# Layer A spectrum: the self-paired rows last, sums and differences on GpSimd, last evictions on two engines

## Chip, cores, metric

The kernel runs on one core of one Trainium2 chip. The metric is device time of one execution in microseconds (us). I call the TensorE matmul engine PE, VectorE DVE, ScalarE ACT, and GpSimd also POOL, as the profile does.

## The reference, cut to what matters

```python
def _A_ref(x, w_r, w_i):                       # x: 1 x 2048 x 640
    X = jnp.fft.rfft2(x.astype(jnp.float32), axes=(-2, -1))
    X = X * (w_r + 1j * w_i)                   # 2048 x 321 weights
    return jnp.fft.irfft2(X, s=(S, D), axes=(-2, -1)).astype(jnp.bfloat16)
...
x = x + _A_ref(_layernorm(x), ...)             # layer A1
x = x + _B_ref(_layernorm(x), ...)             # layer B1 (attention with memory; not changed)
x = x + _A_ref(_layernorm(x), ...)             # layer A2
x = x + _B_ref(_layernorm(x), ...)             # layer B2 (not changed)
```

Layer A is computed with matmuls against Fourier tables. Its middle, `spectrum()`, works through eight groups of rows. Group 0 holds the rows whose mirror is in the same group ("self-paired"); it needs fewer sums than the other seven. After it, `tokens()` needs the result of all eight groups, so the whole of `spectrum()` is on the critical path, in both layers A.

## The kernel before: the parts that matter

An eviction is the copy of a result of PE from PSUM to SBUF. All of this is in `spectrum()`; PE, ACT and DVE run in the order written, GpSimd in an order that a scheduler chooses (here also the order written).

```python
def along_d(j, o):          # 10 matmuls on PE into PSUM tile ab0 or ab1; for o == 1 ACT copies the result out
def combine(j):             # DVE: a+b and a-b, one operand in PSUM, one in SBUF (for j == 0 two copies, one on DVE, one on ACT)
def across(j, sg):          # PE: 4 matmuls into PSUM tile X, of which there is only one
def filt(j, sg):            # DVE: two multiplies of X (PSUM) by the weights (SBUF), into t1, t2
    ...
def products(j, sum_engine):
    sd[j] = quads[2 + j % 3]
    t1, t2 = ts[j % 2]
    a = sd[j].rearrange("p (c s) f -> p c s f", c=2) if j == 0 else acs[j % 2]
    nc.vector.tensor_tensor(out=a[:, 0, :, :], in0=t1[:, :, 0, :], in1=t2[:, :, 0, :], op=ALU.subtract)   # L326
    nc.gpsimd.tensor_tensor(out=a[:, 1, :, :], in0=t1[:, :, 1, :], in1=t2[:, :, 1, :], op=ALU.add)        # L327
    if j:
        sum_engine.tensor_tensor(out=sd[j][:, 0:2, :], in0=a[:, :, 0, :], in1=a[:, :, 1, :], op=ALU.add)  # L329
        nc.gpsimd.tensor_tensor(out=sd[j][:, 2:4, :], in0=a[:, :, 0, :], in1=a[:, :, 1, :], op=ALU.subtract)  # L330

def back(j):                # the inverse transform of group j
    for ch, (f0, f1) in enumerate(CH):                         # three chunks of the 321 frequencies
        psu = pp.tile([128, 2, 2, 128], FP32, tag="pu", bufs=2)  # one PSUM tile for both halves
        ...                                                    # 4 matmuls
        for e in range(2):                                     # two evictions of one half each
            nc.scalar.copy(out=UT[0:m, ch, e, :, j * 16:j * 16 + 16]..., in_=psu[0:m, e, :, :]...)

for j in range(8 + 3):
    if j < 8:       along_d(j, 1)
    if 1 <= j <= 8: across(j - 1, 0); filt(j - 1, 0)
    if j < 8:       along_d(j, 0); combine(j)
    if 1 <= j <= 8: across(j - 1, 1)
    if j >= 3:      back(j - 3)
    if 1 <= j <= 8: filt(j - 1, 1); products(j - 1, nc.vector if j >= 7 else nc.gpsimd)
```
(laid out more tightly than in the file; loads of weights and tables are cut)

Of the kernel before, what the change touches and what calls it, by code (L numbers as in the profile page):

```python
# [13 lines left out]
ALU = mybir.AluOpType  # L14
# [6 lines left out]
NF = 321  # L21
# [76 lines left out]
def _gate(nc, dst1, src1):  # L98
    nc.scalar.copy(out=dst1, in_=src1)
# [36 lines left out]
class _Cut:  # L136

    def __init__(self, t):
        self.t, self.o = t, 0
# [38 lines left out]

class LayerA:

    def __init__(self, tc, g, ar, w_r, w_i, lname):
        self.tc, self.g, self.ar, self.lname = tc, g, ar, lname
        self.w = (w_r, w_i)
        self.wv = [w.rearrange("(p g) f -> p g f", g=16) for w in self.w]
# [17 lines left out]
            nc.gpsimd.indirect_dma_start(out=self.Wm[:, i, :], out_offset=None, in_=w.rearrange("(p g) f -> p (g f)", g=16),  # L202
                                         in_offset=bass.IndirectOffsetOnAxis(ap=self.g["mirror"][:, 0:1], axis=0), element_offset=9 * NF)

    def load_w(self, j):
        nc, W = self.tc.nc, self.W
        W[j, 0] = self.wts[j % 3]
        if j:
            W[j, 1] = self.Wm[:, :, (7 - j) * NF:(8 - j) * NF]
        for i in range(2):  # L210
            nc.sync.dma_start(out=W[j, 0][:, i, :], in_=self.wv[i][:, j, :])
# [49 lines left out]
    def spectrum(self, late_loads=()):  # L261
        tc, g, YT, Fd, K = self.tc, self.g, self.YT, self.Fd, self.K
        nc, W = tc.nc, self.W
        self.UT = UT = self.ar.get("S3", f"{self.lname}UT").bf(3, 2, 16, 128)
        s1 = self.ar.get("S1", f"{self.lname}tmp")
        quads = [s1.bf(4, NF) for _ in range(5)]
        ts = [[s1.f32(2, 2, NF) for _ in range(2)] for _ in range(2)]
        dbs = s1.f32(2, NF)
        W[0, 1] = s1.bf(2, NF)
        for i in range(2):  # L270
            nc.sync.dma_start(out=W[0, 1][:, i, :], in_=self.wv[i][:, 8, :])
        s6 = self.ar.get("S6", f"{self.lname}gt")
        self.Gd = Gd = s6.bf(3, 2, NF)
        self.Ti = Ti = s6.bf(16, 2, 128)
        acs = [s6.f32(2, 2, NF) for _ in range(2)]
        late = [lambda gt: (_gate(nc, Gd[0:1, 0, 0, 0:1], gt), nc.sync.dma_start(out=Gd, in_=g["cd"]["cGd"]))]
        for hf in range(2):
            late.append(lambda gt, hf=hf: (_gate(nc, Ti[0:1, 8 * hf, 0, 0:1], gt),
                                           nc.sync.dma_start(out=Ti[:, 8 * hf:8 * hf + 8], in_=g["cd"]["cTi"][:, 8 * hf:8 * hf + 8])))
        late += list(late_loads)  # L280
        pp = tc.alloc_tile_pool(name=f"{self.lname}_ps2", bufs=1, space=PSUM)
        Kf = K.rearrange("p a b -> p (a b)")
        ab, P, X, sd = {}, {}, {}, {}
        CH = [(0, 128), (128, 256), (256, NF)]

        def along_d(j, o):
            ab[j, o] = ps = pp.tile([128, 2, 512], FP32, name=f"ab{o}", tag=f"ab{o}")
            for ch in range(5):
                for c in range(2):
                    nc.tensor.matmul(ps[:, 1 - c if o else c, 0:NF], lhsT=YT[:, ch, 2 * j + c, :, :].rearrange("p s k -> p (s k)"), rhs=Fd[:, ch, o, :],  # L290
                                     start=(ch == 0), stop=(ch == 4))
            if o == 1 and j:
                ab[j, o] = dbs
                nc.scalar.copy(out=dbs, in_=ps[:, :, 0:NF])

        def combine(j):
            P[j] = quads[j % 2]
            ac, db = ab[j, 0], ab[j, 1]
            if j == 0:
                nc.scalar.copy(out=P[j][:, 2:4, :], in_=db[:, :, 0:NF])  # L300
                nc.vector.tensor_copy(out=P[j][:, 0:2, :], in_=ac[:, :, 0:NF])
                return
            nc.vector.tensor_tensor(out=P[j][:, 0:2, :], in0=ac[:, :, 0:NF], in1=db, op=ALU.add)
            nc.vector.tensor_tensor(out=P[j][:, 2:4, :], in0=ac[:, :, 0:NF], in1=db, op=ALU.subtract)

        def across(j, sg):
            X[j, sg] = x = pp.tile([128, 2, 512], FP32, name="X", tag="X")
            if j == 0:
                a, b = (0, 3) if sg == 0 else (1, 2)
                k = 4 + 3 * sg  # L310
                ops = [(0, k, a), (0, k + 1, b), (1, k + 1, a), (1, k + 2, b)]
            else:
                ops = [(0, 2, 0), (0, 3, 3), (1, 2, 3), (1, 1, 0)] if sg == 0 else [(0, 2, 2), (0, 3, 1), (1, 0, 1), (1, 3, 2)]
            for i, (o, k, p) in enumerate(ops):
                nc.tensor.matmul(x[:, o, 0:NF], lhsT=K[:, k, :], rhs=P[j][:, p, :], start=(i % 2 == 0), stop=(i % 2 == 1))

        def filt(j, sg):
            x = X[j, sg]
            for t, xv, i in ((ts[j % 2][0], x[:, :, 0:NF], 0), (ts[j % 2][1], x[:, ::-1, 0:NF], 1)):
                nc.vector.tensor_tensor(out=t[:, sg, :, :], in0=xv, in1=W[j, sg][:, i, :].unsqueeze(1).to_broadcast([128, 2, NF]), op=ALU.mult)  # L320

        def products(j, sum_engine):
            sd[j] = quads[2 + j % 3]
            t1, t2 = ts[j % 2]
            a = sd[j].rearrange("p (c s) f -> p c s f", c=2) if j == 0 else acs[j % 2]
            nc.vector.tensor_tensor(out=a[:, 0, :, :], in0=t1[:, :, 0, :], in1=t2[:, :, 0, :], op=ALU.subtract)  # L326
            nc.gpsimd.tensor_tensor(out=a[:, 1, :, :], in0=t1[:, :, 1, :], in1=t2[:, :, 1, :], op=ALU.add)  # L327
            if j:
                sum_engine.tensor_tensor(out=sd[j][:, 0:2, :], in0=a[:, :, 0, :], in1=a[:, :, 1, :], op=ALU.add)  # L329
                nc.gpsimd.tensor_tensor(out=sd[j][:, 2:4, :], in0=a[:, :, 0, :], in1=a[:, :, 1, :], op=ALU.subtract)  # L330

        def back(j):
            for ch, (f0, f1) in enumerate(CH):
                m = f1 - f0
                psu = pp.tile([128, 2, 2, 128], FP32, name="psu2", tag="pu", bufs=2)
                if j == 0:
                    for c in range(2):
                        for part in range(2):
                            nc.tensor.matmul(psu[0:m, :, c, :], lhsT=sd[j][:, 2 * part + c, f0:f1], rhs=K[:, 10 + 4 * c + 2 * part:12 + 4 * c + 2 * part, :],
                                             start=(part == 0), stop=(part == 1))  # L340
                else:
                    for e, ops in enumerate((((0, 256), (3, 128)), ((1, 0), (2, 128)))):
                        for i, (o, k) in enumerate(ops):
                            nc.tensor.matmul(psu[0:m, e, :, :], lhsT=sd[j][:, o, f0:f1], rhs=Kf[:, k:k + 256], start=(i == 0), stop=(i == 1))
                for e in range(2):
                    nc.scalar.copy(out=UT[0:m, ch, e, :, j * 16:j * 16 + 16].rearrange("p s (c k) -> p s c k", c=2),
                                   in_=psu[0:m, e, :, :].rearrange("p c (s k) -> p s c k", k=8))

        with tc.manual_schedule(engines={nc.tensor.engine, nc.scalar.engine, nc.vector.engine}):
            for j in range(8 + 3):  # L350
                if j < 8:
                    along_d(j, 1)
                if 1 <= j <= 8:
                    across(j - 1, 0)
                    filt(j - 1, 0)
                if j < 8:
                    along_d(j, 0)
                    combine(j)
                if 1 <= j <= 8:
                    across(j - 1, 1)  # L360
                if j >= 3:
                    back(j - 3)
                    for _ in range(2):
                        if late:
                            late.pop(0)(UT[0:1, 0, 0, 0, (j - 3) * 16:(j - 3) * 16 + 1])
                if 1 <= j <= 8:
                    filt(j - 1, 1)
                    products(j - 1, nc.vector if j >= 7 else nc.gpsimd)
                    if j + 2 < 8:
                        self.load_w(j + 2)  # L370
            for f in late:
                f(UT[0:1, 0, 0, 0, 112:113])
        pp.release()
# [419 lines left out]
def _b_fast_pass(tc, g, bs, env, flag_col, nxt=None):  # L793
# [31 lines left out]
    if True:  # L825
# [196 lines left out]
        with tc.manual_schedule(engines={nc.tensor.engine, nc.scalar.engine, nc.vector.engine}):  # L1022
            for h in range(H + 2):
                if h < H and h % 2 == 0:
                    w = load_w(h // 2)
                    Vt[h // 2] = Vs[h // 2 % 2]
# [389 lines left out]
```

## Time and profile before

| | before |
|---|---|
| median of the first 3 runs | 1668.94 us |
| PE busy over the span | 94% |
| spectrum of A1 (PE starts it; tokens stage starts) | 36.15 to 99.40 us |
| spectrum of A2 | 852.29 to 914.88 us |
| one row group in mid stage | 6.72 us |

The page's first line and its first line on busy time (busy us, share, instructions of each engine):

```profile
span 1669.1 us, 36193 instructions
...
PE 1564.6 (94%) x14240; PEld 1081.5 (65%) x14241; DVE 810.9 (49%) x2308; ACT 837.0 (50%) x2534; POOL 268.5 (16%) x192
```

PE at 94% does not say that PE is the limit everywhere. The view of busy time by stretch, for the second spectrum (window, its length, then busy us and instructions of PE, weight loads, DVE, ACT, POOL, then granted clock, DMA share, GB/s):

```profile
852.00:915.00 63.00, 48.21 (x321) 32.18 (x322) 48.80 (x57) 20.75 (x60) 32.09 (x24) 0.94 0.13 39
```

PE and DVE are each busy for less than 49 of 63 us. What limits the stage must be read from who waits for whom. The DVE timeline of one row group (start, length, engine, line, operation, output from inputs, shape, count):

```profile
882.43 1.55 DVE L320 TENSOR_TENSOR A2tmp_S<-X,A2tab_S 128x642 f32<-128x642 f32 x2
883.90 0.81 DVE L303 TENSOR_TENSOR A2tmp_S<-ab,A2tmp_S 128x642 bf16<-128x642 f32 x1
884.64 0.81 DVE L304 TENSOR_TENSOR A2tmp_S<-ab,A2tmp_S 128x642 bf16<-128x642 f32 x1
885.37 1.54 DVE L320 TENSOR_TENSOR A2tmp_S<-X,A2tab_S 128x642 f32<-128x642 f32 x2
887.02 2.20 DVE L326 TENSOR_TENSOR A2gt_S<-A2tmp_S 128x642 f32<-128x642 f32 x1
889.14 1.55 DVE L320 TENSOR_TENSOR A2tmp_S<-X,A2tab_S 128x642 f32<-128x642 f32 x2
```

From first filter (L320) to first filter is 6.71 us. DVE has no gap over 0.1 us in it. L326, the difference of products, takes 2.20 us. GpSimd's timeline of the same time:

```profile
886.99 1.54 POOL L327 TENSOR_TENSOR A2gt_S<-A2tmp_S 128x642 f32<-128x642 f32 x1 [1.71 <-DVE A2tmp_S L320]
889.39 1.32 POOL L329 TENSOR_TENSOR A2tmp_S<-A2gt_S 128x642 bf16<-128x642 f32 x1 [0.85 <-DVE A2gt_S L326]
```

GpSimd's sum L327 started 0.03 us ahead of L326. Both operations read two tensors in SBUF. There are 16 such pairs in the two layers. In the eight in which DVE started ahead, for instance at 907.99 us below, L326 took 0.83 us and GpSimd's sum 2.05 to 2.21 us; in the eight in which GpSimd started ahead, by 0.02 to 0.03 us, the sum took 1.54 to 1.57 us and L326 2.20 to 2.22 us, ending 0.68 to 0.69 us after the sum. So the one that started second was the longer for it; below I say that it stalled.

The end of the stage, on DVE and on PE:

```profile
906.39 1.56 DVE L320 TENSOR_TENSOR A2tmp_S<-X,A2tab_S 128x642 f32<-128x642 f32 x2 [1.35 <-PE X L315]
907.99 0.83 DVE L326 TENSOR_TENSOR A2gt_S<-A2tmp_S 128x642 f32<-128x642 f32 x1
910.26 0.83 DVE L329 TENSOR_TENSOR A2tmp_S<-A2gt_S 128x642 bf16<-128x642 f32 x1 [1.44 <-POOL A2gt_S L327]
```

```profile
905.10 1.25 PE L315 MATMUL X<-A2tmp_S,A2tab_S 128*128 128x321 bf16 x4 [4.00 <-DVE A2tmp_S L320]
...
914.88 3.38 PE L393 MATMUL psg<-A2gt_S,A2UT_S 128*128 128x321 bf16 x12 [0.73 <-ACT A2UT_S L346]
```

The last filter starts at 906.39 us, the last products end at 912.26, and the tokens stage starts at 914.88 (L393). PE waited 4.00 us for the filter ahead of its last across-matmuls (L315), and these four took 1.25 us where they take 0.72 in mid stage.

### The profile page before, as it was taken

How to read it: one execution, taken by the hardware profiler on the slowest of the kernel's cores; microseconds unless marked ns; L12 is line 12 of the kernel's file. 1: busy time of each engine (PE TensorE's matmuls, PEld its weight loads, DVE VectorE, ACT ScalarE, POOL GpSimd, SP SyncE). 2: the span in 40 equal slices, each digit the busy share in tenths (PEclk: the TensorE clock that was granted, in tenths of full speed). 3: DMA queues.
4: the chain of work that ended last, by engine and by line, in shares of the span. 5: the costliest groups of instructions: out<-in, count | busy, mean ns of one | idle time of the engine just before them, and what ended most of it. 6: DMA issues, size and time to landing. Idle time of an engine off the chain costs nothing. (4 is left out here: it accounts for less than half of the span.)

```text
span 1669.1 us, 36193 instructions
## 1 busy us (share of the span) xinstructions
PE 1564.6 (94%) x14240; PEld 1081.5 (65%) x14241; DVE 810.9 (49%) x2308; ACT 837.0 (50%) x2534; POOL 268.5 (16%) x192
## 2 busy tenths in 40 slices
PE   4887999999999999999987889999999999999998
PEld 2555666666666666677754666676666666666775
DVE  5963354545555554543357724545555554544111
ACT  5364466666666666511123636666666666663000
POOL 0510111121212121100025001121212121111000
PEclk9997999999999999999999999999999999999999
DMA  4463134434343344633301803434343343437241
GB/s 154 158 237 104 51 137 135 151 114 162 112 161 127 137 147 139 227 129 100 91 17 58 283 2 106 148 116 162 112 160 129 135 149 136 136 123 233 66 127 55
DMA packets 167873, 218.05 MB, mean 131 GB/s; under 512 B 7374, under 2 KB 141836, under 8 KB 159756
## 3 DMA queue, kind: packets, MB, share of 16 engines
q1 hardware_dynamic: 167084, 213.34, 38.2%
q8 instruction: 113, 1.85, 0.4%
q0 software_dynamic: 608, 2.30, 0.4%
q14 instruction: 68, 0.56, 0.1%
HBM read 170.52 MB, written 45.09 MB: 129 GB/s over the span
## 5 line engine op out<-in xcount | busy, mean ns | idle before, releaser
L840 PEld LDWEIGHTS <-bB_S 128*128 128x128 bf16 x3180 | 260.3, 97 | 187.1 <-issue 7.8
L984 DVE TENSOR_TENSOR bB_S<-pso,bB_S 128x480 bf16<-128x480 f32 (+1 forms) x320 | 189.5, 593 | 264.7 <-PE pso L975 249.1
L919 ACT ACTIVATE bB_S<-pss 128x269 bf16<-128x269 f32 (+5 forms) x576 | 213.3, 385 | 192.6 <-PE pss L916 177.8
L1134 PE MATMUL psx<-Wo_sb,bB_S 128*128 128x320 bf16 x2048 | 288.2, 299 | 2.9 <-DMA bB_S<-oTx_d 2.9
L1134 PEld LDWEIGHTS <-bB_S 128*128 128x128 bf16 x2048 | 197.2, 98 | 79.5 <-DMA bB_S<-oTx_d 3.6
L899 DVE CAST bB_S<-psk 128x495 bf16<-128x495 f32 (+3 forms) x320 | 191.4, 599 | 115.9 <-PE psk L840 85.6
L920 DVE TENSOR_TENSOR bB_S<-bB_S,maskf 128x269 bf16<-128x269 bf16 (+5 forms) x576 | 163.1, 287 | 152.6 <-ACT bB_S L919 148.8
L944 POOL TENSOR_TENSOR bB_S<-bB_S,bB_S 128x634 f32<-128x634 f32 x64 | 98.2, 1535 | 821.1 <-ACT bB_S L940 821.1
L908 ACT CAST bB_S<-psv 128x512 bf16<-128x512 f32 (+1 forms) x288 | 160.5, 557 | 84.0 <-PE psv L906 83.7
L884 ACT ACTIVATE bB_S<-psq 128x480 bf16<-128x480 f32 x300 | 152.6, 509 | 98.2 <-PE psq L840 98.2
L840 PE MATMUL psk<-B2hT_S,bB_S 128*128 128x495 bf16 (+3 forms) x800 | 165.0, 342 | 3.7 <-DVE bB_S L899 2.5
L840 PE MATMUL psk<-B1hT_S,bB_S 128*128 128x495 bf16 (+3 forms) x800 | 165.0, 342 | 1.8 <-DVE B1hT_S L1219 1.2
L906 PE MATMUL psv<-bB_S,B2hT_S 128*128 128x256 bf16 x1360 | 163.4, 272 | 0.2 <-DVE bB_S L899 0.2
L906 PE MATMUL psv<-bB_S,B1hT_S 128*128 128x256 bf16 x1360 | 163.4, 272 | 0.2 <-DVE bB_S L899 0.2
L916 PEld LDWEIGHTS <-bB_S 128*128 128x128 bf16 x1216 | 103.0, 98 | 90.1 <-issue 6.4
L840 PE MATMUL psq<-B1hT_S,bB_S 128*128 128x495 bf16 (+5 forms) x780 | 157.6, 336 | 0.1
L840 PE MATMUL psq<-B2hT_S,bB_S 128*128 128x495 bf16 (+5 forms) x780 | 157.6, 336 | 0.1
L916 PE MATMUL pss<-bB_S 128*128 128x132 bf16 (+8 forms) x1216 | 148.3, 216 | 3.1
L906 PEld LDWEIGHTS <-B1hT_S 128*128 128x128 bf16 x1360 | 128.6, 98 | 13.7 <-issue 0.3
L906 PEld LDWEIGHTS <-B2hT_S 128*128 128x128 bf16 x1360 | 128.5, 98 | 13.8 <-issue 0.3
L975 PE MATMUL pso<-bB_S,bB_S 128*128 128x132 bf16 (+8 forms) x1216 | 119.6, 216 | 0.0
L975 PEld LDWEIGHTS <-bB_S 128*128 128x128 bf16 x1216 | 91.2, 98 | 15.7 <-DVE oTmf L985 0.5
(223 smaller groups left out, 1565.7 us busy)
## 6 DMA issues: line engine op xcount, KB each, us to landing
bB_S<-Rd SPq DMA_DIRECT2D x62, 1059.5 KB
oTx_d<-bB_S SPq DMA_DIRECT2D x60, 512.0 KB
bB_S<-oTx_d SPq DMA_DIRECT2D x56, 512.0 KB
bB_S<-in_B_Wq_dram SPq DMA_DIRECT2D x32, 320.0 KB
bB_S<-in_B_Wk_dram SPq DMA_DIRECT2D x32, 320.0 KB
bB_S<-in_B_Wv_dram SPq DMA_DIRECT2D x32, 320.0 KB
bB_S<-oTx_d SPq DMA_DIRECT2D x14, 384.0 KB
Wo_sb<-in_B_Wo_dram SPq DMA_DIRECT2D x4, 1280.0 KB
```

The source lines that it names most:

```text
L840: nc.tensor.matmul(ps, lhsT=w[:, ch, hh * 128:(hh + 1) * 128], rhs=src[:, ch, lo:hi], start=(ch == 0), stop=(ch == 4))
L884: nc.scalar.mul(out=qv[:, :, 0:SEG], in_=x_view(ps, o, n)[:, :, 1:SW], mul=scale)
L899: nc.vector.tensor_copy(out=KTs[h % 2][:, lo:hi], in_=ps[:, 0:hi - lo])
L906: nc.tensor.matmul(ps[:, i * 256:(i + 1) * 256], lhsT=hT[:, ch, (t + i) * 128:(t + i + 1) * 128], rhs=w["Wv"][:, ch, :], start=(ch == 0), ...
L908: nc.scalar.copy(out=V[:, t:t + n, :].rearrange("p a b -> p (a b)"), in_=ps[:, 0:n * 256])
L916: nc.tensor.matmul(ps[:, off - o0:off - o0 + hi - lo], lhsT=KT[:, t * 128:(t + 1) * 128], rhs=QT[:, lo:hi], start=True, stop=True)
L919: nc.scalar.activation(out=E[:, 0:n], in_=ps[:, 0:n], func=ACTF.Exp)
L920: nc.vector.tensor_tensor(out=P[:, o0:o0 + n], in0=E[:, 0:n], in1=bs.mask[:, o0:o0 + n], op=ALU.mult)
L944: nc.gpsimd.tensor_tensor(out=accS, in0=accS, in1=sums_sb, op=ALU.add)
L975: nc.tensor.matmul(pso[:, lo - q0:hi - q0], lhsT=V[:, t, (h % 2) * 128:(h % 2 + 1) * 128], rhs=P[:, off:off + hi - lo], start=(i == 0), st ...
L984: nc.vector.tensor_tensor(out=oT.rearrange("p (r s j) -> p r s j", r=16, j=2)[:, :, s0:s0 + ns, :], in0=byclass(po), in1=rx, op=ALU.mult)
L1134: self.tc.nc.tensor.matmul(ps[:, 0:320], lhsT=lhs(h, k // 2), rhs=self.g["Wo_sb"][:, h, c0:c0 + 320], start=(h == 0), stop=(h == H - 1))
```

## The change

The intent: take L326 from DVE in mid stage; let the last group be the self-paired one, which needs just two operations after its filters, on DVE; and divide the last evictions between ACT and DVE.

```diff
+    SEQ = (1, 2, 3, 4, 5, 6, 7, 0)
 ...
+        pos = {j: p for p, j in enumerate(self.SEQ)}
 ...
-        def products(j, sum_engine):
+        def products(j):
 ...
-            nc.vector.tensor_tensor(out=a[:, 0, :, :], ..., op=ALU.subtract)
-            nc.gpsimd.tensor_tensor(out=a[:, 1, :, :], ..., op=ALU.add)
+            (nc.gpsimd if pos[j] < 6 else nc.vector).tensor_tensor(out=a[:, 0, :, :], ..., op=ALU.subtract)
+            (nc.gpsimd if j else nc.vector).tensor_tensor(out=a[:, 1, :, :], ..., op=ALU.add)
             if j:
-                sum_engine.tensor_tensor(out=sd[j][:, 0:2, :], ..., op=ALU.add)
+                nc.gpsimd.tensor_tensor(out=sd[j][:, 0:2, :], ..., op=ALU.add)
                 nc.gpsimd.tensor_tensor(out=sd[j][:, 2:4, :], ..., op=ALU.subtract)
 ...
-                    nc.scalar.copy(out=UT[...], in_=psu[0:m, e, :, :]...)
+                    (nc.vector.tensor_copy if j == 0 and e else nc.scalar.copy)(out=UT[...], in_=psu[0:m, e, :, :]...)
 ...
-            for j in range(8 + 3):
+            for i in range(8 + 3):
+                j, last = [self.SEQ[k] if 0 <= k < 8 else None for k in (i, i - 1)]
```
(cut: buffers and weight loads are numbered by position instead of by group, and the loop body uses `j`, `last` and `done = self.SEQ[i - 3]`)

Line numbers shift by it: filters L320 → L324, combines L303/L304 → L307/L308, products L326/L327/L329/L330 → L330/L331/L333/L334, across L315 → L319, inverse L339/L344 → L343/L348, evictions L346 → L350, first matmuls of the tokens stage L393 → L399.

More of the change, by code (lines that the diff above doesn't have):

```diff
@@ L203, in tables, with load_w @@
                                          in_offset=bass.IndirectOffsetOnAxis(ap=self.g["mirror"][:, 0:1], axis=0), element_offset=9 * NF)
-    def load_w(self, j):
-        nc, W = self.tc.nc, self.W
-        W[j, 0] = self.wts[j % 3]
+    def load_w(self, p):
+        nc, W, j = self.tc.nc, self.W, self.SEQ[p]
+        W[j, 0] = self.wts[p % 3]
         if j:
@@ L294, in along_d @@
                 nc.scalar.copy(out=dbs, in_=ps[:, :, 0:NF])
+        pos = {j: p for p, j in enumerate(self.SEQ)}
         def combine(j):
-            P[j] = quads[j % 2]
+            P[j] = quads[pos[j] % 2]
             ac, db = ab[j, 0], ab[j, 1]
@@ L318, in filt @@
             x = X[j, sg]
-            for t, xv, i in ((ts[j % 2][0], x[:, :, 0:NF], 0), (ts[j % 2][1], x[:, ::-1, 0:NF], 1)):
+            for t, xv, i in ((ts[pos[j] % 2][0], x[:, :, 0:NF], 0), (ts[pos[j] % 2][1], x[:, ::-1, 0:NF], 1)):
                 nc.vector.tensor_tensor(out=t[:, sg, :, :], in0=xv, in1=W[j, sg][:, i, :].unsqueeze(1).to_broadcast([128, 2, NF]), op=ALU.mult)
-        def products(j, sum_engine):
-            sd[j] = quads[2 + j % 3]
-            t1, t2 = ts[j % 2]
-            a = sd[j].rearrange("p (c s) f -> p c s f", c=2) if j == 0 else acs[j % 2]
-            nc.vector.tensor_tensor(out=a[:, 0, :, :], in0=t1[:, :, 0, :], in1=t2[:, :, 0, :], op=ALU.subtract)
-            nc.gpsimd.tensor_tensor(out=a[:, 1, :, :], in0=t1[:, :, 1, :], in1=t2[:, :, 1, :], op=ALU.add)
+        def products(j):
+            sd[j] = quads[2 + pos[j] % 3]
+            t1, t2 = ts[pos[j] % 2]
+            a = sd[j].rearrange("p (c s) f -> p c s f", c=2) if j == 0 else acs[pos[j] % 2]
+            (nc.gpsimd if pos[j] < 6 else nc.vector).tensor_tensor(out=a[:, 0, :, :], in0=t1[:, :, 0, :], in1=t2[:, :, 0, :], op=ALU.subtract)
+            (nc.gpsimd if j else nc.vector).tensor_tensor(out=a[:, 1, :, :], in0=t1[:, :, 1, :], in1=t2[:, :, 1, :], op=ALU.add)
             if j:
-                sum_engine.tensor_tensor(out=sd[j][:, 0:2, :], in0=a[:, :, 0, :], in1=a[:, :, 1, :], op=ALU.add)
+                nc.gpsimd.tensor_tensor(out=sd[j][:, 0:2, :], in0=a[:, :, 0, :], in1=a[:, :, 1, :], op=ALU.add)
                 nc.gpsimd.tensor_tensor(out=sd[j][:, 2:4, :], in0=a[:, :, 0, :], in1=a[:, :, 1, :], op=ALU.subtract)
@@ L345, in back @@
                 for e in range(2):
-                    nc.scalar.copy(out=UT[0:m, ch, e, :, j * 16:j * 16 + 16].rearrange("p s (c k) -> p s c k", c=2),
-                                   in_=psu[0:m, e, :, :].rearrange("p c (s k) -> p s c k", k=8))
+                    (nc.vector.tensor_copy if j == 0 and e else nc.scalar.copy)(out=UT[0:m, ch, e, :, j * 16:j * 16 + 16].rearrange("p s (c k) -> p s c k", c=2),
+                                                                                in_=psu[0:m, e, :, :].rearrange("p c (s k) -> p s c k", k=8))
         with tc.manual_schedule(engines={nc.tensor.engine, nc.scalar.engine, nc.vector.engine}):
-            for j in range(8 + 3):
-                if j < 8:
+            for i in range(8 + 3):
+                j, last = [self.SEQ[k] if 0 <= k < 8 else None for k in (i, i - 1)]
+                if j is not None:
                     along_d(j, 1)
-                if 1 <= j <= 8:
-                    across(j - 1, 0)
-                    filt(j - 1, 0)
-                if j < 8:
+                if last is not None:
+                    across(last, 0)
+                    filt(last, 0)
+                if j is not None:
                     along_d(j, 0)
                     combine(j)
-                if 1 <= j <= 8:
-                    across(j - 1, 1)
-                if j >= 3:
-                    back(j - 3)
+                if last is not None:
+                    across(last, 1)
+                if i >= 3:
+                    done = self.SEQ[i - 3]
+                    back(done)
                     for _ in range(2):
                         if late:
-                            late.pop(0)(UT[0:1, 0, 0, 0, (j - 3) * 16:(j - 3) * 16 + 1])
-                if 1 <= j <= 8:
-                    filt(j - 1, 1)
-                    products(j - 1, nc.vector if j >= 7 else nc.gpsimd)
-                    if j + 2 < 8:
-                        self.load_w(j + 2)
+                            late.pop(0)(UT[0:1, 0, 0, 0, done * 16:done * 16 + 1])
+                if last is not None:
+                    filt(last, 1)
+                    products(last)
+                    if i + 2 < 8:
+                        self.load_w(i + 2)
             for f in late:
```

## The prediction

> **What bounds the kernel now.** The page gives PE 94% of a 1669.1 us span. The change touches only the two spectrum stages of layer A: 36–99 and 852–915 us (timeline). There PE is busy about 49 of 63 us, DVE 49, ACT 21, POOL 32 (busy time by stretch), and the chain of waits runs through DVE: filters and the difference of products (L326).
>
> In mid stage a row group takes 6.72 us (filters of the second spectrum start at 875.69, 882.43, 889.14, 895.86). DVE does 4 filters and 2 combines at 0.74 us pitch (4.5 us), and L326 at 2.2 us. Alone L326 takes 0.83 us; it reads two SBUF tensors while GpSimd's sum (L327, 1.55 us) does too[...]. Filters and combines, with one operand in PSUM, keep 0.81 us beside GpSimd, and GpSimd's 1.32 us stays.
>
> **What the change does.**
> 1. L326 moves from DVE to GpSimd for six row groups. GpSimd then needs 2 × 1.55 + 2 × 1.30 = 5.7 us per group: below the new period, with two iterations of slack before the inverse transform.
> 2. Not all 2.2 us come off: X has one buffer, so the next group's across-matmuls wait for the last filter, and PE has inverse matmuls and along_d ahead of them. Filter 1.61 + across 0.57 + inverse 1.76 + along_d 1.38 + across and latency 0.81 = 6.13 us. The period goes 6.72 → 6.13; the first two groups stay at 5.37 (L326 was hidden). About 2.4 us per layer, less 0.5: the first group now has two combines.
> 3. Before, L326 and a DVE sum stood before the last group's filters (gap 7.63 us); now one difference, 0.8 to 2.2 us, and a shorter combine: about 5.6 us, gain 1.5 to 2.
> 4. The last products took 907.99 to 912.26 us; the self-paired group needs two DVE operations, 1.6 us: gain 2.7.
> 5. The last evictions on two engines: about 0.4 of the 2.6 us from last product to the tokens stage.
>
> Sum: about 6 us per layer, 12 us in all, all critical, since the tokens stage needs every row group. A further 0 to 1.5 us: PE idles 4.0 us before the last across-matmuls, and matmuls after it run near half speed; the second layer's first 12 tokens matmuls take 3.38 us against 1.83 in the first layer.[...]
>
> **Predicted: 1656.5 us, 8 in 10 between 1651.0 and 1662.5.** Faster by over 2%: 1%; within 2%: 98%; slower: 1%. Stage B is unchanged and follows earlier.
>
> **Signs.** DVE idles about 0.8 us before each group's first filter, released by X; filter starts 6.1 us apart; POOL busy about 42 us per spectrum (32 before), nearly back to back; last products 1.6 us; each spectrum about 57 us.
>
> **What would make it wrong.** GpSimd slower than 1.55 us per operation when fed continuously: above 6.1 us per group it is the bound and its backlog ends the stage. A stall of the DVE difference of group seven behind that backlog. A cold PE at the end (1 to 2 us per layer). The first spectrum waiting for mirrored weights, needed one group earlier; they are issued by 18 us, needed at 46, so I doubt it.

The five items were put at about 6 us a layer, 12 us in all, with 0 to 1.5 us more for a shorter wait of PE, and 1656.5 is 12.4 us below the 1668.94 of before. The trace of before showed PE slow after a wait of 4.00 us (four across-matmuls 1.25 us instead of 0.72).

## The result

| | before | after |
|---|---|---|
| median | 1668.90 us (4 runs, 1668.41 to 1673.11) | 1658.55 us (4 runs, 1656.54 to 1660.01) |
| ratio | | 0.9932, 95% interval 0.9912 to 0.9951 |
| PE start to tokens stage, A1 | 63.25 us | 58.13 us |
| PE start to tokens stage, A2 | 62.59 us | 58.18 us |

A ratio is the mean time of one kernel's runs over that of the other's runs of the same rounds, so it is not quite the ratio of the medians. Executions over 1.5% slower than the fastest of the same kernel are left out of the means. The interval lies below 1, so about 10 us are gained.

The same lines of the page and of busy time by stretch, after:

```profile
span 1658.3 us, 36195 instructions
...
PE 1563.1 (94%) x14240; PEld 1081.0 (65%) x14241; DVE 790.0 (48%) x2300; ACT 835.6 (50%) x2528; POOL 282.4 (17%) x206
```

```profile
849.50:906.40 56.90, 47.82 (x316) 31.90 (x315) 39.10 (x53) 19.78 (x56) 38.54 (x31) 0.93 0.14 43
```

DVE's work fell by 9.7 us in the spectrum and GpSimd's rose by 6.5 us. A row group in mid stage, on DVE and on GpSimd:

```profile
879.01 1.56 DVE L324 TENSOR_TENSOR A2tmp_S<-X,A2tab_S 128x642 f32<-128x642 f32 x2 [1.63 <-issue]
880.48 0.82 DVE L307 TENSOR_TENSOR A2tmp_S<-ab,A2tmp_S 128x642 bf16<-128x642 f32 x1
881.22 0.82 DVE L308 TENSOR_TENSOR A2tmp_S<-ab,A2tmp_S 128x642 bf16<-128x642 f32 x1
881.95 1.55 DVE L324 TENSOR_TENSOR A2tmp_S<-X,A2tab_S 128x642 f32<-128x642 f32 x2
885.13 1.56 DVE L324 TENSOR_TENSOR A2tmp_S<-X,A2tab_S 128x642 f32<-128x642 f32 x2 [1.63 <-issue]
```

```profile
877.75 1.54 POOL L330 TENSOR_TENSOR A2gt_S<-A2tmp_S 128x642 f32<-128x642 f32 x1
879.25 1.58 POOL L331 TENSOR_TENSOR A2gt_S<-A2tmp_S 128x642 f32<-128x642 f32 x1
880.91 1.33 POOL L333 TENSOR_TENSOR A2tmp_S<-A2gt_S 128x642 bf16<-128x642 f32 x1
882.20 1.32 POOL L334 TENSOR_TENSOR A2tmp_S<-A2gt_S 128x642 bf16<-128x642 f32 x1
```

From filter to filter it is now 6.12 us (879.01 to 885.13). DVE waits 1.63 us in each group (the profile names no releaser), and GpSimd works almost without a gap. PE in the same group:

```profile
880.62 0.72 PE L319 MATMUL X<-A2tmp_S,A2tab_S 128*128 128x321 bf16 x4 [0.34 <-DVE A2tmp_S L324]
881.18 1.04 PE L348 MATMUL psu<-A2tab_S,A2tmp_S 128*128 128x256 bf16 x8
882.52 0.60 PE L348 MATMUL psu<-A2tab_S,A2tmp_S 128*65 128x256 bf16 x4 [0.30 <-ACT A2UT_S L350]
882.95 1.54 PE L292 MATMUL ab<-A2tab_S,A2YT_S 128*128 128x321 bf16 x10
884.33 0.71 PE L319 MATMUL X<-A2tmp_S,A2tab_S 128*128 128x321 bf16 x4
```

The loop can be read off from start to start: filter (879.01), across (880.62), inverse (881.18), along_d (882.95), across (884.33), next filter (885.13). That is 1.61 + 0.56 + 1.77 + 1.38 + 0.80 = 6.12 us, and the last across-matmuls end 0.09 us before the filter. The end of the stage:

```profile
895.29 0.84 DVE L330 TENSOR_TENSOR A2gt_S<-A2tmp_S 128x642 f32<-128x642 f32 x1
...
898.74 1.56 DVE L324 TENSOR_TENSOR A2tmp_S<-X,A2tmp_S 128x642 f32<-128x642 f32 x2 [1.13 <-PE X L319]
900.34 0.83 DVE L330 TENSOR_TENSOR A2tmp_S<-A2tmp_S 128x642 bf16<-128x642 f32 x1
901.08 0.82 DVE L331 TENSOR_TENSOR A2tmp_S<-A2tmp_S 128x642 bf16<-128x642 f32 x1
904.41 0.96 DVE L350 CAST A2UT_S<-psu 128x256 bf16<-128x256 f32 x2 [2.51 <-ACT A2UT_S L350]
905.93 0.42 DVE L350 CAST A2UT_S<-psu 65x256 bf16<-65x256 f32 x1 [0.56 <-ACT A2UT_S L350]
```

```profile
897.67 1.03 PE L319 MATMUL X<-A2tmp_S,A2tab_S 128*128 128x321 bf16 x4 [1.71 <-DVE A2tmp_S L324]
898.50 3.33 PE L348 MATMUL psu<-A2tab_S,A2tmp_S 128*128 128x256 bf16 x16
...
903.36 1.14 PE L343 MATMUL psu<-A2tab_S,A2tmp_S 128*128 128x256 bf16 x8 [0.19 <-ACT A2UT_S L350]
...
906.40 1.83 PE L399 MATMUL psg<-A2gt_S,A2UT_S 128*128 128x321 bf16 x12 [0.91 <-DVE A2UT_S L350]
```

```profile
901.34 2.50 ACT L350 CAST A2UT_S<-psu 65x256 bf16<-65x256 f32 x8 [0.25 <-PE psu L348]
904.00 0.37 ACT L350 CAST A2UT_S<-psu 128x256 bf16<-128x256 f32 x1 [0.16 <-PE psu L343]
```

The last products end at 901.90 us, 3.16 us after the start of the last filter (before: 5.87). But the tokens stage (L399) starts only 4.50 us after that (before: 2.62).

To add it up I cut the stage into parts between marks that every trace shows. The stage length from here on is counted from the first combine on DVE (a copy in the kernel before) to the first tokens-stage matmul. For the second layer:

| part, us | before | after | after, second profile (e5) |
|---|---|---|---|
| first combine to first filter | 1.87 | 2.22 | 2.22 |
| first filters of group 1 to group 7 (six gaps) | 37.03 | 35.23 | 35.23 |
| gap to the last group's first filter | 7.63 | 4.79 | 4.79 |
| last group, first to second filter pair | 2.90 | 2.69 | 2.38 |
| second filter pair to the end of the last products | 5.87 | 3.16 | 3.21 |
| last products to tokens stage | 2.62 | 4.50 | 3.62 |
| stage | 57.92 | 52.59 | 51.45 |

The first layer's stage went from 57.91 to 52.52. The two together gained 10.72 us, and the spans of the two profiles differ by 10.8. Counted from PE's start the second layer gained less, 4.41 us: its first 30 matmuls took 6.88 us after and 5.95 before, and the granted clock was 0.50 until 853.57 us after, but only from 853.33 to 856.74 before.

Everything outside the two stages does not hold so still. Subtracting both stages from the profiled span leaves 1553.27 us before and 1553.19 after, but over all 14 profiles told here it runs from 1547.4 to 1553.4, for the same instructions. So kernel times carry a few us of noise from stage B, while stage lengths repeat to about 0.1 us up to the last group. I judge parts of the change by the stage and use the kernel time as a check.

### The profile page after: what moved, and what is told of

It reads as the page before. It is cut to its first block, busy times and chain, and to the rows that moved or that the text cites. A ratio compares the mean times of both kernels' runs of the same rounds, so it can differ in the third digit from the quotient of the medians.

```text
span 1658.3 us, 36195 instructions
## 1 busy us (share of the span) xinstructions
PE 1563.1 (94%) x14240; PEld 1081.0 (65%) x14241; DVE 790.0 (48%) x2300; ACT 835.6 (50%) x2528; POOL 282.4 (17%) x206
```

## The experiments

The first four ran on one chip with shared runs of before, so did the next four, then three, then one. Ratios are against before.

### e1: the order alone

```diff
 # against the changed kernel
-            (nc.gpsimd if pos[j] < 6 else nc.vector).tensor_tensor(out=a[:, 0, :, :], ...
-            (nc.gpsimd if j else nc.vector).tensor_tensor(out=a[:, 1, :, :], ...
+            nc.vector.tensor_tensor(out=a[:, 0, :, :], ...
+            nc.gpsimd.tensor_tensor(out=a[:, 1, :, :], ...
-                nc.gpsimd.tensor_tensor(out=sd[j][:, 0:2, :], ...
+                (nc.vector if pos[j] >= 6 else nc.gpsimd).tensor_tensor(out=sd[j][:, 0:2, :], ...
 # evictions all on ACT
```

> Only the order of the row groups changes (self-paired last); difference on VectorE and evictions on ScalarE as before. Stage length is counted from the first VectorE combine to the first matmul of the tokens stage (57.9 us before, 52.5 to 52.6 after). My theory: the parts add up; the period of a row group stays 6.7 us, the last products shrink from 4.3 to about 2.2 us, of which some is given back to inverse matmuls queued behind: stage 56 to 56.7 us, kernel about 3 us faster. Rival, that the order is what the gain is about: stage near 53 us and the kernel 8 to 10 us faster.

Measured: 1667.71 us, ratio 0.9990 (0.9977 to 1.0002); stages 57.46 and 57.47 us. Filter gaps were 6.70 to 6.73 us in mid stage, from the third gap on; in the kernel before the third is 6.14 to 6.18, because there DVE's difference started 0.05 us ahead of GpSimd's sum and took 0.83 us. The last products took 3.83 us from the last filter, 2.0 less than before, but the tokens stage then came 3.88 us later instead of 2.62. So the order alone is worth 0.45 us a layer, less than my 1.2 to 1.9. The rival falls. As a kernel time the gain is not shown: the interval includes 1.

### e2: the move to GpSimd alone

```diff
 # against the kernel before
-            nc.vector.tensor_tensor(out=a[:, 0, :, :], ...
+            (nc.gpsimd if j < 6 else nc.vector).tensor_tensor(out=a[:, 0, :, :], ...
```

> Only the difference of products goes to GpSimd, for the first six row groups; order and evictions as before. My theory: filter starts in mid stage 6.13 us apart rather than 6.72 in three gaps, the gap before the last group and everything after as before: stage about 56.1 us, kernel about 3.6 us faster. If GpSimd were the bound, filter starts would be 5.7 us apart or its backlog would lengthen the end. Rival, that the move is what the gain is about: stage near 53 us.

Measured: 1664.70 us, ratio 0.9973 (0.9960 to 0.9986); stages 56.40 and 56.17 us. Three gaps of 6.7 became 6.12 to 6.13; the last gap (7.65) and the end (5.88 and 2.62) stayed to 0.02 us. This is as my theory said: 1.5 to 1.75 us a layer.

The order alone gives 0.45 us and the move alone about 1.6, and together with the split evictions they give 5.3 to 5.4. The parts do not add: in both single runs the seventh group's difference still stalls before the last group's filters (last gap 7.08 and 7.65), and in the changed kernel it does not (4.79), because there DVE also lost the seventh group's sum, and GpSimd, still busy with the sixth group's L334 and four memsets of stage B, starts its sum 0.50 us after DVE's difference (895.79 and 895.29 us); in e1 and e2 the two start within 0.03 us of each other. That this order came out so well is luck: the prediction allowed 0.8 to 2.2 us for it.

### e3: the last evictions on ACT alone

```diff
-                    (nc.vector.tensor_copy if j == 0 and e else nc.scalar.copy)(out=UT...
+                    nc.scalar.copy(out=UT...
```

> The changed kernel with the last six evictions on ScalarE alone. Theory: ScalarE is at work from about 901.3 us of the second spectrum on, so three more evictions of 0.33 us each cost 0.5 to 1 us per layer: stage 53.0 to 53.6 us, kernel 1 to 2 us slower than the changed one. Rival, PE's queue alone sets the end: no change (stage 52.5 to 52.7).

Measured: 1655.99 us, ratio 0.9919 (0.9905 to 0.9933); stages 51.06 and 52.33 us. Undoing the split did not cost anything; both theories missed. The two layers differ by 1.27 us although they run the same code: in the first the across-matmuls after the 1.71 us wait took 0.72 us, in the second 1.13. From the last products to the tokens stage it took 3.26 us with PE at speed and 4.13 with a slow PE. The changed kernel, in the same two conditions, shows 3.62 (e5) and 4.50. So the split on two engines costs 0.36 to 0.37 us instead of gaining.

### e4: the sixth group's inverse ahead of the last across

```diff
-                if last is not None:
+                if last is not None and i < 8:
                     across(last, 1)
                 if i >= 3:
                     done = self.SEQ[i - 3]
                     back(done)
+                if i == 8:
+                    across(last, 1)
```

> The changed kernel, but in the last iteration PE does the inverse matmuls of the sixth row group before the second across-matmuls of the last group, while it would wait for the filter. Theory 1, that the 1.9 us lost between last products and tokens stage is PE's in-order queue, slowed by its idle time: the wait of 1.7 us is filled, the inverse matmuls no longer run near half speed, stage about 50.7 us (1.9 less), kernel 3 to 4 us faster than the changed one. Theory 2, that ScalarE's evictions in a row (2.5 us without a break) set the end: stage 52.0 to 52.6, no more than 1 us faster.

Measured: 1656.62 us, ratio 0.9927 (0.9915 to 0.9939); stages 52.26 and 51.30 us. Theory 1 in this form falls. The 1.71 us wait was filled and the across-matmuls took 0.71 us in both layers, but the end hardly moved: where PE was at speed it took 3.46 us from the last products, against 3.62. PE now waited for GpSimd's two last results of the seventh group instead (0.62 and 1.00 us in the trace). After those waits the first layer's PE was slow again: the seventh group's four 128*65 matmuls took 0.90 us, against 0.60 in the second layer.

### e5: the changed kernel again

> The changed kernel once more, unedited, on the chip of the next three. Kernel 8 to 13 us faster than before, ratio 0.992 to 0.995. Theory of the end: everything up to the second across-matmuls of the last group repeats to 0.1 us; from there on the stage length [...]: 52.5 us where the four across-matmuls take about 1.03 us (as in both spectra of the first profile), about 1.0 to 1.3 us less where they take 0.72 us.

Measured: 1656.47 us, ratio 0.9920 (0.9907 to 0.9934); stages 51.41 and 51.45 us, against 52.52 and 52.59 in its first profile. PE's timeline at the end of the second layer:

```profile
897.44 0.72 PE L319 MATMUL X<-A2tmp_S,A2tab_S 128*128 128x321 bf16 x4 [1.71 <-DVE A2tmp_S L324]
...
905.03 1.83 PE L399 MATMUL psg<-A2gt_S,A2UT_S 128*128 128x321 bf16 x12 [0.91 <-DVE A2UT_S L350]
```

The wait is the same 1.71 us, but the four across-matmuls take 0.72 us instead of 1.03, and everything up to them repeats. Over all profiles with a wait of exactly 1.71 us here, PE came out slow in four spectra and at speed in five; after the 4.00 us wait of before, e1 and e2 it was slow in six of six.

The granted clock is on record in a trace. In the changed kernel's first profile it was 1.00 from 853.57 to 897.94 us, 0.50 up to 901.36 us, and 1.00 after that. In the traces of before and after, every change (20 records each) lies a multiple of 3.41 us after the first one, so I cut by these. Two stretches of that length from the changed kernel's first profile, then two of e5's (columns as in the view of busy time by stretch; PE busy first, granted clock third from the end):

```profile
894.53:897.94 3.41, 1.46 (x10) 0.92 (x10) 2.99 (x4) 1.38 (x5) 3.33 (x7) 1.00 0.01 2
897.94:901.36 3.42, 3.42 (x18) 2.34 (x16) 2.58 (x4) 1.31 (x5) 2.27 (x2) 0.50 0.00 0
894.93:898.35 3.42, 1.71 (x14) 1.04 (x13) 2.51 (x5) 0.75 (x3) 3.34 (x7) 1.00 0.01 2
898.35:901.76 3.41, 2.97 (x23) 2.03 (x21) 3.02 (x4) 2.92 (x10) 1.64 (x2) 1.00 0.00 0
```

In the stretch with the wait PE is busy for 0.43 of the length (1.46 of 3.41 us) in the first profile, and the next stretch is at half the clock. In e5 it is busy for 0.50 (1.71 of 3.41 us), and the next one is at the full clock. The first layer of the first profile repeats it: 1.47 of 3.41 us (82.16 to 85.57), then a clock of 0.50 up to 88.98 us. In the second layer of before, three stretches at full clock were followed by one at half: PE was busy for 1.49 us (849.92 to 853.33), 0.00 (901.12 to 904.53, in the wait of 4.00 us) and 1.60 us (911.36 to 914.77). These are times by the profile, which models the ends of matmuls, and no run varied PE's busy share by itself, so no limit is told from them.

The same wait of 1.71 us was thus followed by either clock. What differs between the two profiles above is where the stretches lie: in the first the stretch also takes in most of a 0.30 us gap that PE has just before (PE restarts at 894.77), in e5 it starts after that gap. That this is what decided was not shown.

### e6: the last evictions divided by PSUM tile

```diff
-                    (nc.vector.tensor_copy if j == 0 and e else nc.scalar.copy)(out=UT...
+                    (nc.vector.tensor_copy if j == 0 and ch == 1 else nc.scalar.copy)(out=UT...
```

> The changed kernel, but the last group's evictions are divided by PSUM tile (the second of three to VectorE, the others to ScalarE) instead of by halves of one tile. Theory, that VectorE's half waits for ScalarE's [...]: VectorE's evictions no longer wait for ScalarE, the end from last products to tokens stage falls from 4.5 to 3.7 to 4.1 us with a slow PE and to 3.0 to 3.3 with a full-speed one, kernel 1 to 2 us faster than the changed one. Rival, that the two engines wait because they write the same tile of the result: VectorE still waits for ScalarE and nothing is gained.

Measured: 1656.83 us, ratio 0.9934 (0.9920 to 0.9947); stages 51.04 and 52.54 us (at speed in the first layer, across-matmuls 0.73 us; slow in the second, 1.26 us after a wait of 2.03 us). DVE's eviction, first layer:

```profile
89.86 0.76 DVE L350 CAST A1UT_S<-psu 128x256 bf16<-128x256 f32 x2 [1.84 <-PE psu L343]
```

It is released by PE, not by ACT, and its two evictions take 0.76 us together. In the changed kernel DVE's evictions (904.41 and 905.93 us above) are released by ACT's eviction of the other half: ACT's took 0.37 us, and DVE's 0.42 followed it. Two halves in series on two engines take longer than two in a row on ACT (0.65 us together in the traces, where they overlap). The end from the last products is 3.26 us at speed: 0.36 less than the changed kernel, and the same as with ACT alone in e3. So the theory, that DVE's half waits because it shares a PSUM tile with ACT's, holds against the rival, the tile of the result. The releasers are semaphores, so the wait is one that the built program contains, not one that the chip was seen to impose. Dividing the work gains nothing over one engine. As a kernel time none of this shows within the interval.

### e7: a third of the inverse moved into PE's wait

```diff
+                done = self.SEQ[i - 3] if i >= 3 else None
+                if 3 <= i < 8:
+                    back(done, (0,))
                 if last is not None:
                     across(last, 1)
                 if i >= 3:
-                    back(done)
+                    back(done, (1, 2) if i < 8 else (0, 1, 2))
```

> The changed kernel, but in the middle of the stage the first third of the inverse matmuls goes ahead of the second across-matmuls, where PE waits 0.34 us for a filter. Theory, that the 6.13 us period is the loop filter, across, inverse, along_d, across on PE: filter starts 5.70 to 5.85 us apart (then GpSimd's 5.7 us is next), four gaps, stage 1.2 to 1.7 us shorter per layer (about 51 us with a slow PE at the end), kernel 2 to 3.5 us faster than the changed one. Rival, that GpSimd or VectorE sets the period: it stays at 6.13.

Measured: 1657.15 us, ratio 0.9935 (0.9922 to 0.9949); stages 52.56 and 53.62 us. The mid-stage filter gaps (third to sixth) fell to 5.36 to 5.38 us, which is further than I expected. So PE's loop did set 6.13, and GpSimd, at 5.7 us a group, does not pace the filters over these few groups. Its backlog came out at the end instead, so the stage got no shorter (I expected about 51 us): 5.4 to 5.8 us from last filter to last products (3.16 in the changed kernel) and 5.0 to 6.3 us from there to the tokens stage. PE's timeline, first layer, shows the inverse of the seventh group waiting for GpSimd:

```profile
86.26 0.28 PE L350 MATMUL psu<-A1tab_S,A1tmp_S 128*128 128x256 bf16 x1 [0.77 <-POOL A1tmp_S L333]
88.12 2.37 PE L350 MATMUL psu<-A1tab_S,A1tmp_S 128*128 128x256 bf16 x11 [1.58 <-POOL A1tmp_S L334]
```

### e8: more work on GpSimd

```diff
+                if pos[j] < 6:      # result is read by nobody; 100 columns in layer 1, 321 in layer 2
+                    nc.gpsimd.tensor_tensor(out=dose, in0=a[:, 0, 0, 0:dose.shape[1]], in1=a[:, 1, 0, 0:dose.shape[1]], op=ALU.add)
```

> The changed kernel with one more GpSimd operation after each of the first six groups, whose result nobody reads: 100 columns (about 0.3 us) in the first layer, 321 (about 0.8 us) in the second. Theory, that GpSimd is not the bound of the period: filter starts stay 6.13 us apart in both layers, as GpSimd has two row groups of slack; first layer's stage the same within 0.5 us; in the second GpSimd's backlog comes out at the end, stage about 2 us longer. Rival, that GpSimd at 5.7 us plus waits paces the filters: filter starts about 0.3 us further apart in the first layer and 0.4 to 0.8 us in the second.

Measured: 1663.57 us (one run); stages 53.48 and 57.09 us. The mid-stage filter gaps (third to sixth) stayed at 6.12 to 6.17 us in both layers, so GpSimd is not the bound there. The end was more sensitive than I thought: 1.0 us more in the first layer and 4.5 in the second, against 0.5 at most and about 2 expected. The seventh group's difference stalled in both (1.88 and 1.19 us), and in the second layer DVE's last products stalled too (5.96 us from the last filter).

### e9: PE kept busy over the wait

```diff
+        def fill(n):
+            ps = pp.tile([128, 2, 512], FP32, name="ab0", tag="ab0")
+            for k in range(n):
+                nc.tensor.matmul(ps[:, k % 2, 0:NF], lhsT=K[:, 2, :], rhs=Fd[:, k % 5, 0, :], start=True, stop=True)
 ...
+                if i == 8:
+                    fill(11)
                 if last is not None:
                     across(last, 1)
```

> The changed kernel, with eleven matmuls whose result nobody reads (into PSUM space that is free by then) put where PE waits 1.7 us for the last group's first filter. Theory, [...]: the across-matmuls after it take 0.72 us in both layers, stage 51.4 to 51.5 us in both, kernel 0 to 2 us faster than the changed one on average. Rival, that the slow matmuls come from something else (a fixed window of time): some spectra still show 1.0 us or more there and a stage of 52.5 us.

Measured: 1652.16 us, ratio 0.9890 (0.9875 to 0.9906), runs 1650.51 to 1653.43; stages 51.40 and 51.44 us. PE's timeline, second layer:

```profile
891.12 1.67 PE L356 MATMUL ab<-A2tab_S 128*128 128x321 bf16 x11
892.99 0.72 PE L319 MATMUL X<-A2tmp_S,A2tab_S 128*128 128x321 bf16 x4 [0.21 <-DVE A2tmp_S L324]
...
900.58 1.83 PE L406 MATMUL psg<-A2gt_S,A2UT_S 128*128 128x321 bf16 x12 [0.91 <-DVE A2UT_S L350]
```

The wait is down to 0.21 us, the across-matmuls take 0.72 us in both layers, and both stages have the length of e5. Two spectra at speed alone would prove little, as five of nine were so with the wait in place. But the across-matmuls took 0.71 to 0.73 us in all eight spectra in which this wait was filled (e4, e9, e11, e12), and in e9, from the filling matmuls to the tokens stage, PE's longest gap is 0.91 us and it is busy for 0.60 or more of any 3.41 us (by its timelines of both layers). So the slow end is caused by PE's idle time at this wait: with the wait filled, it did not come in any of the eight. (The theory expected 0.72 us and 51.4 to 51.5 us.) The rival, a fixed window of time, expected some spectra at 1.0 us or more, and there were none. The stages explain at most 2.3 us of the gain over the changed kernel; the rest of the 4.3 us between the medians of e5 and e9 is not from the stage, since the rest of this profile was 1548.9 us against 1553.4 in e5's.

### e10 and e11: the divided inverse with less on GpSimd

```diff
 # e10: e7's edit, e6's evictions, and
-            (nc.gpsimd if pos[j] < 6 else nc.vector).tensor_tensor(out=a[:, 0, :, :], ...
+            (nc.gpsimd if 3 <= pos[j] < 6 else nc.vector).tensor_tensor(out=a[:, 0, :, :], ...
 # e11: e10 and e9's eleven filling matmuls
```

> The divided inverse matmuls (filter starts 5.37 us apart), with the difference of products back on VectorE for the first three groups, where VectorE waits 0.87 us for X anyway and GpSimd has time, and the last evictions divided by PSUM tile. Theory, that with the shorter period GpSimd's backlog is what ends the stage: 3 x 1.5 us less of it gives a stage of 48.0 to 50.5 us, kernel 13 to 17 us faster than before. If VectorE's difference stalls on GpSimd in these groups, filter starts go back to about 6.1 us and nothing is gained over the changed kernel.

> As the run before it, with the eleven filling matmuls: stage 48.0 to 49.5 us in both layers, with the across-matmuls after the wait at 0.72 us, kernel 14 to 18 us faster than before. If its end is set by GpSimd alone, it equals the run before it.

Measured: e10 1656.61 us, ratio 0.9916 (0.9903 to 0.9930), stages 52.34 and 52.64; e11 1655.63 us, ratio 0.9912 (0.9897 to 0.9927), stages 52.57 and 52.58. Both missed. DVE's first two differences in e10, second layer, took 0.83 us each (858.02 and 863.33 us); the third:

```profile
868.77 2.21 DVE L330 TENSOR_TENSOR A2gt_S<-A2tmp_S 128x642 f32<-128x642 f32 x1
```

The first two fit into DVE's wait and cost nothing. The third started together with GpSimd's sum and took 2.21 us, which made that gap 6.73 us. With the end 4.7 us from last filter to last products, GpSimd was still behind. The filling matmuls in e11 changed nothing, as PE went idle again later, waiting for GpSimd (0.50 and 1.58 us for the seventh group's L333 and L334 in the first layer).

### e12: two differences on DVE, and filling matmuls in two places

```diff
 # e11, but
+            (nc.gpsimd if 2 <= pos[j] < 6 else nc.vector).tensor_tensor(out=a[:, 0, :, :], ...
+                if i in (8, 9):
+                    fill(11 if i == 8 else 8)
```

> Divided inverse matmuls, difference of products on VectorE for the first two groups only (the third stalled 2.21 us), on GpSimd for the next four, evictions divided by PSUM tile, eleven filling matmuls before the last group's second across-matmuls and eight before the seventh group's inverse matmuls. Theory, that GpSimd's backlog is now what ends the stage: filter starts 5.37 us apart throughout, GpSimd done with the seventh group about 1.9 us sooner than in the run with three, stage 49.8 to 50.8 us in both layers, kernel 18 to 21 us faster than before. Rival, that the end is set by PE and ScalarE behind it: stage 51.0 to 51.5, no better than the changed kernel with filling matmuls.

Measured: 1652.34 us, ratio 0.9891 (0.9874 to 0.9907), runs 1651.61 to 1654.08; stages 50.58 and 50.60 us, the shortest of all. The filter gaps were 5.31 to 5.37 us throughout, as expected, and the stage is in the expected range, though the gap to the last group was 5.28 to 5.30 us (4.79 in the changed kernel), since the seventh group's difference stalled behind GpSimd. The stage is 0.8 us a layer shorter than e9's, outside the rival's range. In kernel time it is no better than e9 (0.9891 and 0.9890, from different rounds); 1.7 us for both layers is less than either interval resolves.

## Why the prediction was right, and where a step of it failed

The prediction said 1656.5 us, and 1658.55 and (in e5) 1656.47 were measured. It said 6 us a layer and up to 1.5 more in all; the stages gained 5.3 to 5.4 us a layer with a slow PE at the end and 6.5 with PE at speed. That it came so close is partly luck. The five items add up to 6.5 to 7.0 us a layer, and the last gap gained 0.8 to 1.3 us more than said, which made up for part of step 5, off by 2.3. Step by step:

1. "GpSimd then needs 2 × 1.55 + 2 × 1.30 = 5.7 us per group": measured 5.7 us, and e8 shows that it is not the bound of mid stage. The sign "about 42 us per spectrum" was a wrong sum of right terms: six groups at 5.7 and 4.4 us for the seventh are 38.6, and 38.54 was measured.
2. "The period goes 6.72 → 6.13": measured 6.12 to 6.13. The mechanism, PE's order, is shown by e7: moving four matmuls of inverse work on PE changed the period to 5.37 with no change on GpSimd or DVE; and the five terms of the sum were met to 0.01 us (PE's timeline above). What the one X tile adds is argued: no run gave X a second buffer. The size of the gain was off: only three gaps had been at 6.7 us, not four, so it gave 1.8 us, not 2.4. The sign for DVE's idle time was also off: it is 0.82 to 0.87 us only before the inverse matmuls begin, and 1.63 us after, which is 6.13 less the 4.5 us of work that the prediction itself named.
3. The gap to the last group went to 4.79 us, not 5.6: gain 2.84 us, as the seventh group's difference did not stall (0.84 us).
4. The last products gained 2.71 us; predicted 2.7.
5. "The last evictions on two engines: about 0.4 of the 2.6 us" is the step that failed. The end after the last products did not shrink but grew, to 4.50 us, or 3.62 with PE at speed. What it had wrong is the overlap: the two halves were not copied at the same time but one after the other, ACT 0.37 us and then DVE 0.42. Of the 1.88 us that the end grew, 0.88 come from the slow PE (4.50 against 3.62), 0.36 from the split, and 0.64 remain. First, the split: the two halves share a PSUM tile, and DVE's eviction of one is released by ACT's of the other; this costs 0.36 us (e3 and e6 against the changed kernel, at equal PE speed). On ACT alone the two halves took 0.65 us. Why the built program keeps the two apart was not shown; no run let them overlap. Second, the 0.64 us, where the cause is argued: the products now end sooner than PE, ACT and GpSimd have done the groups before: with PE at speed and evictions on ACT alone, ACT's 18 evictions of the first layer in e3 run without a break for 5.97 us. Even then the end takes 3.26 us, and the old 2.62 does not come back. In e4 it was GpSimd's last results that PE waited for. How the 0.64 us divide among PE, ACT and GpSimd I have not measured.
6. "A cold PE at the end (1 to 2 us per layer)", listed as a risk, came true in the first profile: 1.1 us per layer. After both of its 1.71 us waits the granted clock was 0.50 for 3.41 us (from 85.57 and from 897.94 us). A wait of 1.71 us was followed by a slow PE in four spectra of nine (four across-matmuls 1.02 to 1.26 us instead of 0.72), and e9 removes the slow matmuls by filling the wait. So the hope that a shorter wait would keep PE at speed held for only part of the runs. The 12 first tokens-stage matmuls, 3.38 us in the second layer of the first profile, took 1.83 us in both layers after.

The stall of DVE and GpSimd on each other, which the change was built on, is in the traces: 0.83 against 2.20 to 2.22 us for L326, and 1.54 to 1.57 against 2.05 to 2.21 us for GpSimd's sum when DVE started first. DVE's combines, with one operand in PSUM, took 0.81 to 0.82 us with GpSimd at work too (L303 and L304 before). GpSimd's L333 and L334 took 1.32 us at the same 642 columns as its products of 1.55 us. Their result is bf16, but that is not it: group 0's two operations in e2 write bf16 as well and took 1.54 to 1.55 us. L333 and L334 read both inputs from one tile, the others from two; no run tests whether that is the cause. What no run isolated is why stage B, with the same instructions, varies by up to 6 us between profiles. The mean granted clock of the profile does not tell: it was 0.987 both in the changed kernel's first profile, where the rest is 1553.19 us, and in e7, where it is 1547.4. That stays open.

## What to carry to other kernels

When an operation moves off a saturated engine, the gain is the old period less the period of the next loop (here 0.6 us a group for an operation of 2.2 us), so look for the next loop, and count the groups that really ran at the old period. Work given to GpSimd, off the critical path, cost nothing here in mid stage (filter gaps of 6.12 to 6.17 us in e8 with an operation more) and came out at the end, where its backlog was the last thing that anybody waited for (1.0 and 4.5 us more). Here two engines that evicted halves of one PSUM tile took turns (0.37 us, then 0.42), and a wait of 1.71 us of PE was followed, in four spectra of nine, by across-matmuls of 1.02 to 1.26 us instead of 0.72. So check both wherever a stage ends on a few short operations.
